# Moving one step's output products from the last single slot to the head of the first slot of two steps

## The chip, the core and the metric

The kernel runs on one core of a Trainium2 chip. The metric is the device time of one execution in microseconds (us). The engines are named as in the profile: PE is TensorE (matmuls; PEld its weight loads), DVE is VectorE, ACT is ScalarE, POOL is GpSimd, and SP is SyncE, which here issues most of the DMAs.

## The reference

Windowed attention with block summaries runs ahead of a gated network without a nonlinearity. What is computed:

```python
# q, k, v: (4, 8, 768, 64); block 32, window 16
k_sum = k.reshape(B, H, nb, block, D).max(axis=3)
v_sum = v.reshape(B, H, nb, block, D).mean(axis=3)
scores_l = scale * q @ k^T            # kept where |i - j| < window
scores_s = scale * q @ k_sum^T + log(block)
a = softmax(concat(scores_l, scores_s))
attn = a @ concat(v, v_sum)           # -> x: 3072 tokens x 512
a = x @ w1;  b = x @ w2               # 512 x 1024 each
out = ((a * b) @ w3) @ w_out          # 1024 x 1024, 1024 x 512
```

## The kernel before, in words

**Two streams of work share PE.** The attention is cut into 24 steps (6 units of 512 tokens by 4 pairs of heads). A step consists of its scores (`scores`, L383: 32 small matmuls into two PSUM banks), the masked minimum and the exponentials (`reduce` on DVE, L397; `expose` on ACT, L411), the normalization (`normalize` on ACT, L421), the transposes (`transposes`, L441: 16 matmuls into two banks), their copy to SBUF (`evacuate`, L449 and L451, both on ACT here), and the outputs (`outputs`, L464: 32 small matmuls into one bank), which `finish_step` follows with a copy out of PSUM (`keep_raw` on ACT, L484). The network is a stream of 128x512 matmuls (L128, and L747 for the products of a fast scheme with seven products instead of eight). `run` puts a given number of that stream's columns between the parts of the steps.

**The order on PE is the order in which the code calls.** PE, SP and POOL run in the order of the code; ACT and DVE do so inside the blocks marked `manual_schedule(engines=VECTOR)` for the calls of those blocks, while other work (weight casts, copies of the stream) is merged in by a scheduler. From step 8 on, steps 8 to 15 have a slot each (`lump`), and steps 16 to 23 go two to a slot (`two_steps`). In `lump(p)` the outputs of step p - 3 come first, then the transposes of p - 2 and the scores of p. In `two_steps(8)`, the first of its kind, come the transposes of step 14, whatever outputs of steps 12 and 13 are still open, and the scores of steps 16 and 17; the outputs of 14, the transposes and the outputs of 15 stand further down.

**PSUM banks.** Eight banks are dealt out in rings by tag: two for "mm", two for "tp", four for "sc". The ring "sc" holds the scores (two banks a step), the outputs of the later steps (`SPARE`), and every third accumulator of the network's second unit (`bank(wide)`). Just ahead of the place at hand the ring goes: outputs of step 12, two for the scores of 15, the accumulator `mm_2858`, outputs of 13, two for the scores of 16, two for the scores of 17. So the second bank of step 17's scores is the one that the outputs of step 13 had: PE may write it when the copy of L484 has read it.

**DMA lanes.** Each DMA issued by SP or ACT signals its landing on one of eight semaphores (`DMAHW0` to `DMAHW7` in the lists of order below), which the program deals out in turn. Before it issues a DMA, the issuing engine waits until the last DMA of that lane has landed; what stands behind on that engine waits too. On ACT this concerns `project`, which sends its results out from ACT (L562, behind the copy of L561).

**Values.** `load_values` (L332, three DMAs) and `fetch_means` (L366) fill a step's tile `v`, of which there are two; the loads of step 15 reuse the tile of step 13 and go when the outputs of 13 are through. The weights of the fast scheme stream in through `flow_in` (L792, tile `ws`).

Of the kernel before, what the change touches and what calls it, by code (L numbers as in the profile page):

```python
# [76 lines left out]
def attention_moe(ctx, tc, qG, kW, kT, vP, vW, vB, mask, w1, w2, w3T, wo, out, outT):  # L77
# [241 lines left out]
    def batches(u):  # L319

        for b in range(B):
            at, to = max(0, b * BLOCKS - u * NBLK), min(NBLK, (b + 1) * BLOCKS - u * NBLK)
            if at < to:
                yield b, slice(at, to), to - at

    def load_values(u, p):


        v = sb.tile([P, 2, NBLK, P], F32, name="v", bufs=2)

        for g, rows in ((0, slice(0, CUT)), (1, slice(0, CUT - 64)), (1, slice(CUT + NB - 64, KR))):
            (nc.gpsimd if u >= LAST_UNITS else nc.sync).dma_start(v[rows, g], vW[u, p, rows, g])  # L332
        return v
# [28 lines left out]
    def fetch_means(u, p, v):  # L362
        for b, blocks, n in batches(u):
            for g, at in enumerate((CUT, CUT - 64)):
                src = vS[b][32 * p : 32 * p + NB]
                nc.sync.dma_start(v[at : at + NB, g, blocks], src.unsqueeze(1).broadcast_to([NB, n, P]))  # L366
# [41 lines left out]
    def expose(h, sm, mx):  # L408
        for i in ORDER:
            j = h * NBLK + i  # L410
            nc.scalar.activation(  # L411
                sm[:, j], sm[:, j], AF.Exp, bias=mx[:, 0, j : j + 1], scale=-1.0, accum_out=mx[:, 1, j : j + 1]
            )
# [20 lines left out]
    def transposes(sm, **more):  # L434

        tp = [ps.tile([P, 512], F32, name="tp", **more or {"bufs": 2}) for _ in range(2)]
        for j in range(NI):
            for g in range(2):
                rows = slice(64 * g, 64 * g + 64)
                to, p = tp[g][:KR, j * 64 : j * 64 + 64], sm[rows, j]  # L440
                nc.tensor.transpose(to, p, ident[rows, rows])  # L441
        return tp

    def evacuate(tp, second="V", home=None):
        if home is None:
            pt = [sb.tile([KR, U], F32, name="pt", bufs=4) for _ in range(2)]
        else:
            pt = [home[:KR, g * U : (g + 1) * U] for g in range(2)]
        nc.scalar.copy(pt[0], tp[0][:KR, :U])  # L449
        if second == "A":  # L450
            nc.scalar.copy(pt[1], tp[1][:KR, :U])  # L451
        else:
            nc.vector.tensor_copy(pt[1], tp[1][:KR, :U])
        return pt
# [571 lines left out]
    def place(s):  # L1026
        return divmod(s, NPAIR)

    inputs, values, sms = {}, {}, {}

    def fetch(s):
        if s < NS:
            inputs[s] = load_scores(*place(s))

    def fetch_values(s):
        if s < NS:
            values[s] = load_values(*place(s))
# [5 lines left out]
    def fill(s):  # L1043
        if s < NS:
            gather(*place(s), inputs[s][1])

    def begin(s):
        u, p = place(s)
        held_in = sb.tile([P, 2 * U], F32, name="sm", tag="wf", bufs=6)
        sm = held_in[:, : NI * KR].rearrange("p (a b) -> p a b", b=KR)  # L1050
        mx = aligned([P, 3, NI], name="mx", bufs=4)
        sms[s] = sm, held_in
        return u, sm, mx, scores(*inputs.pop(s))
# [13 lines left out]
    def load_batch():  # L1067
        for _ in range(2 if later_batches else 0):
            load_, work = later_batches.pop(0)
            under_way.append((work, load_()))  # L1070

    def reduce_batch():
        for work, raw in under_way:
            work(raw)
        under_way.clear()
# [175 lines left out]
    def finish_step(p, pt, **more):  # L1251
        u, c = place(p)
        po = outputs(pt, values.pop(p), **more)
        if u < 2:
            keep_x(po, xs[u])
        else:
            keep_raw(po, u, c)
# [47 lines left out]
    def lump(p):  # L1305

        lag, last = p in LAG, p == SINGLE - 1
        if p == NFIRST:
            load_batch()
            fill(p)  # L1310
        else:
            if p not in LAG or p == LAG[0]:
                fetch_means(*place(p - 1), values[p - 1])
            elif p > LAG[1]:
                fetch_means(*place(p - 2), values[p - 2])
            fetch(p + 1)
        with tc.manual_schedule(engines=VECTOR):
            if p - 3 in turned:
                finish_step(p - 3, turned.pop(p - 3), **SPARE)
            t, home = sms.pop(p - 2)  # L1320
            turned[p - 2] = evacuate(transposes(t), "V" if p in (12, 13) else "A", home)
            u, sm, mx, sc = begin(p)
            reduce(u, 0, sc, sm, mx)
            if p > NFIRST + 1:
                expose(0, sm, mx)
                reduce(u, 1, sc, sm, mx)
        if last:
            fetch(p + 2)
        if lag and p > LAG[0]:
            fetch_values(p - 1)  # L1330
        run(given[0] + (24 if p == NFIRST + 1 else 18) * U)
        with tc.manual_schedule(engines=VECTOR):
            if not lag or last:
                finish_step(p - 2, turned.pop(p - 2), **SPARE)
            if p <= NFIRST + 1:
                expose(0, sm, mx)
                reduce(u, 1, sc, sm, mx)
            expose(1, sm, mx)
            invert(mx)
            normalize(sm, mx)  # L1340
            fill(p + 1)
            reduce_batch()
        if not lag or last:
            fetch_values(p)
        if last:
            fill(p + 2)
        for work in EXTRA.get(p, ()):
            work()
        run((given[0] + UP_TO[p]) / 2)
        load_batch()  # L1350
        run(UP_TO[p])
# [8 lines left out]
    def two_steps(m):  # L1360

        a, b = 2 * m, 2 * m + 1
        first = m == PAIRS[0]
        if first:
            for p in (a - 2, a - 1):
                fetch_means(*place(p), values[p])
        with tc.manual_schedule(engines=VECTOR):
            if first:
                t, home = sms.pop(a - 2)
                pt = evacuate(transposes(t), "A", home)  # L1370
            for p in (a - 4, b - 4):
                if p in turned:
                    finish_step(p, turned.pop(p), **SPARE)
            if m in PAIRS:
                (u, sm, mx, sc), (u2, sm2, mx2, sc2) = [begin(p) for p in (a, b)]
                reduce(u, 0, sc, sm, mx)
                expose(0, sm, mx)
                reduce(u, 1, sc, sm, mx)
        if not first:
            fetch_values(a - 2)  # L1380
        for work in LATER.get((m, 0), ()):
            work()
        if m in PAIRS:
            fetch(a + 2)
            run(given[0] + LEAD / 2)
            with tc.manual_schedule(engines=VECTOR):
                expose(1, sm, mx)
                reduce(u2, 0, sc2, sm2, mx2)
                invert(mx)
            run(given[0] + LEAD / 2)  # L1390
            with tc.manual_schedule(engines=VECTOR):
                if first:
                    finish_step(a - 2, pt, **SPARE)
                    turn((a - 1,), "A")
                expose(0, sm2, mx2)
                reduce(u2, 1, sc2, sm2, mx2)
                if m == PAIRS[0] + 1:
                    first_sums(0)
                normalize(sm, mx)
            if not first:  # L1400
                fetch_values(b - 2)
            fetch(b + 2)
            run(CLASSIC + LAST_SINGLE * FAST if first else (given[0] + begins(m + 1)) / 2)
            with tc.manual_schedule(engines=VECTOR):
                if first:
                    finish_step(a - 1, turned.pop(a - 1), **SPARE)
                expose(1, sm2, mx2)
                invert(mx2)
                normalize(sm2, mx2)
                if m == PAIRS[0] + 2:  # L1410
                    first_sums(1)
        if not first and m - 1 <= PAIRS[-1]:
            with tc.manual_schedule(engines=VECTOR):
                turn((a - 2, b - 2), "A")
        if m not in PAIRS:
            fetch_values(b - 2)
        for p in (a, b):
            fill(p + 2)
            if not first and p - 2 in values:
                fetch_means(*place(p - 2), values[p - 2])  # L1420
        for work in LATER.get((m, 1), ()):
            work()
        run(begins(m + 1))
# [75 lines left out]
```

## Time and profile before

| What | Value |
|---|---|
| Median of 3 runs | 505.38 us (505.33 to 505.58) |
| The profiled execution: its own time | 503.69 us |
| The profiled execution: its span, first to last instruction | 501.9 us |
| PE busy | 482.8 us, 96% of the span |
| ACT busy | 315.6 us, 63% |
| DVE busy | 358.4 us, 71% |

The span is 1.8 us short of the profiled execution's time, and that time is 1.7 us under the median of the runs without a profile. PE's busy share includes waits inside a run of matmuls, since their ends are modelled; how dense PE really is shows in the time from one group's start to the next one's.

### The profile page before, as it was taken

The numbers are of one execution on the slowest core, as the hardware profiler recorded it, in microseconds if no ns is written. First come the engines' busy times: TensorE is split into PE (matmuls) and PEld (weight loads), VectorE is DVE, ScalarE is ACT, GpSimd is POOL, SyncE is SP. The second block draws the span as 40 slices with busy tenths as digits, with TensorE's granted clock in tenths as the row PEclk, the third lists the DMA queues.
The fourth block names the chain that finished last, engine by engine and source line by source line (L and its number), as shares of the span: only waits on it lengthen the run. The fifth ranks groups of instructions, "written<-read, shape, count | busy, mean of one in ns | idle before, by whom it ended". The sixth has DMA issues, their size and how long they took to land.

```text
span 501.9 us, 10535 instructions
## 1 busy us (share of the span) xinstructions
PE 482.8 (96%) x3804; PEld 391.5 (78%) x3804; DVE 358.4 (71%) x874; ACT 315.6 (63%) x874; POOL 70.5 (14%) x131
## 2 busy tenths in 40 slices
PE   0998999999999999999999999999999999999997
PEld 0766778888877888888777888888888888888886
DVE  4879887897714798985559995799967038139972
ACT  5588965677816888887797779489534412413710
POOL 1024533000202110001252131202000000000000
PEclk9999999999999999999999999999999999999999
DMA  8999597999499999989999999997769656565762
GB/s 341 412 406 303 209 352 246 370 400 411 144 315 257 271 277 339 277 255 332 313 341 330 336 369 251 365 281 228 227 173 296 208 200 193 188 196 182 219 200 85
DMA packets 54404, 139.29 MB, mean 278 GB/s; under 512 B 6224, under 2 KB 17232, under 8 KB 51792
## 3 DMA queue, kind: packets, MB, share of 16 engines
q1 hardware_dynamic: 49136, 124.71, 73.1%
q0 software_dynamic: 4064, 11.82, 9.8%
q10 hardware_dynamic: 1152, 2.10, 1.1%
q8 instruction: 30, 0.49, 0.4%
q14 instruction: 22, 0.18, 0.1%
HBM read 105.89 MB, written 32.70 MB: 276 GB/s over the span
## 4 chain that ended last, share of the span: by engine, by line
PE 75%; DVE 9%; ACT 8%; DMA 5%; issue 1%; SPq 1%; ACTq 0%
PE ln L747 41%; PE mm L128 26%; PE po L464 4%; PE sc L383 3%; ACT sm L411 3%; DVE wf L211 2%; DVE w L124 2%; DMA ws<-wS 2%; DMA v<-vS 2%; PE tp L441 2%; ACT w L226 1%; ACT hT L650 1%; DMA k<-in_kW_dram 1%; DMA wraw<-in_wo_dram 1%; DVE wf L208 1%
## 5 line engine op out<-in xcount | busy, mean ns | idle before, releaser
L747 PE MATMUL ln<-xT,ws 128*128 128x512 f32 x672 | 156.7, 392 | 0.1
L747 PEld LDWEIGHTS ln<-xT,ws 128*128 128x128 f32 x672 | 125.0, 188 | 28.9 <-DVE tmp L767 0.8
L128 PE MATMUL mm<-x,w 128*128 128x512 f32 x384 | 89.5, 392 | 0.0
L128 PEld LDWEIGHTS mm<-x,w 128*128 128x128 f32 x384 | 71.4, 188 | 15.7 <-issue 0.8
L411 ACT ACTIVATE sm<-sm,mx 128x120 f32<-128x120 f32 x192 | 74.0, 393 | 11.7 <-DVE mx L397 11.6
L747 PE MATMUL ln<-hT,ws 128*128 128x512 f32 (+1 forms) x348 | 77.6, 383 | 0.1
L767 DVE TENSOR_TENSOR tmp<-ln,tmp 128x512 f32<-128x512 f32 (+1 forms) x53 | 35.6, 681 | 53.8 <-PE ln L747 39.7
L747 PEld LDWEIGHTS ln<-hT,ws 128*128 128x128 f32 x348 | 63.6, 188 | 13.3 <-ACT tmp L765 0.6
L128 PE MATMUL mm<-w,w 128*128 128x512 f32 x192 | 50.5, 414 | 14.7 <-ACT w L226 11.4
L650 ACT CAST hT<-hr 128x512 fp32r<-128x512 f32 x56 | 32.1, 625 | 40.7 <-DVE hr L824 32.0
L128 PEld LDWEIGHTS mm<-w,w 128*128 128x128 f32 x192 | 36.5, 196 | 25.6 <-ACT w L226 11.8
L397 DVE CUSTOM_DVE_ANT_0 sm<-sc,mask_sb 128x120 f32<-128x120 f32 x192 | 41.3, 278 | 15.3 <-PE sc L383 15.3
L128 PE MATMUL mm<-wp,h 128*128 128x512 f32 x192 | 45.7, 394 | 0.0
L128 PEld LDWEIGHTS mm<-wp,h 128*128 128x128 f32 x192 | 35.6, 188 | 8.3 <-issue 0.5
L421 ACT ACTIVATE sm<-sm,mx 128x120 f32<-128x120 f32 x128 | 39.3, 395 | 2.4 <-DVE mx L417 2.4
L124 DVE TENSOR_TENSOR hT<-hr,hT 128x512 fp32r<-128x512 f32 x56 | 35.9, 696 | 3.9 <-ACT hT L650 3.9
L411 ACT ACTIVATION_READ_ACCUMULATOR sm<-sm,mx 128x1 f32 x192 | 37.8, 197 | 0.0
L124 DVE TENSOR_TENSOR w<-wf,w 128x1024 fp32r<-128x1024 f32 (+1 forms) x22 | 26.4, 1200 | 8.0 <-ACT w L226 7.9
L226 ACT CAST w<-wf 128x1024 fp32r<-128x1024 f32 (+1 forms) x22 | 21.3, 969 | 15.6 <-DVE wf L211 14.3
L370 POOL COPY k<-ks 128x96 f32<-128x96 f32 (+1 forms) x32 | 11.2, 363 | 135.6 <-DMA k<-in_kW_dram 110.8
L765 ACT COPY tmp<-ln 128x512 f32<-128x512 f32 x32 | 18.8, 590 | 14.9 <-PE ln L747 13.7
L181 ACT ACTIVATE wf<-wraw 128x1024 f32<-128x1024 f32 (+1 forms) x22 | 23.1, 1061 | 6.6 <-DMA wraw<-in_wo_dram 3.6
(73 smaller groups left out, 578.5 us busy)
## 6 DMA issues: line engine op xcount, KB each, us to landing
ws<-wS SPq DMA_DIRECT2D x56, 512.0 KB
wraw<-in_w3T_dram SPq DMA_DIRECT2D x8, 1024.0 KB
wraw<-in_w_dram SPq DMA_DIRECT2D x8, 1024.0 KB
wS<-sp SPq DMA_DIRECT2D x16, 512.0 KB
ws<-pS SPq DMA_DIRECT2D x16, 512.0 KB
raw<-in_kT_dram SPq DMA_DIRECT2D x16, 392.0 KB
wS<-w SPq DMA_DIRECT2D x12, 512.0 KB
ws<-pW SPq DMA_DIRECT2D x24, 256.0 KB
```

Of the source, the lines that this page charges most:

```text
L124: eng.tensor_tensor(dst, src, hi.bitcast(F32), ALU.subtract)
L128: nc.tensor.matmul(acc, lhsT=a, rhs=b, start=first and i == 0, stop=last and i == len(terms) - 1)
L181: nc.scalar.activation(f[:, some], words[:, some, 1].bitcast(F32), AF.Prelu, scale=2.0**-112, alpha=-(2.0**32),)
L226: nc.scalar.copy(t[:, 0, some], f[:, some])
L397: nc.vector.tensor_tensor_reduce(out=sm[:, j], in0=sc[h][:, i * KR : (i + 1) * KR], in1=mask_sb[:, 0 if blk == 0 else 2 if blk == BLOCKS - ...
L411: nc.scalar.activation(sm[:, j], sm[:, j], AF.Exp, bias=mx[:, 0, j : j + 1], scale=-1.0, accum_out=mx[:, 1, j : j + 1])
L421: nc.scalar.activation(sm[:, j], sm[:, j], AF.Copy, scale=mx[:, 2, j : j + 1])
L464: nc.tensor.matmul(po[cols, at : at + 64], lhsT=v[:KR, g, i, cols], rhs=pt[g][:, (h * NBLK + i) * 64 : (h * NBLK + i + 1) * 64], start=Tru ...
L650: nc.scalar.copy(dst[0], src)
L747: nc.tensor.matmul(bank[:, cols], lhsT=x, rhs=y[:, cols], start=c + j == 0 and (split or k in o.first), stop=c == steps - 1 and j == 2 and ...
L765: nc.scalar.copy(parts[to][:, cols], got)
L767: nc.vector.tensor_tensor(parts[to][:, cols], got, parts[more][:, cols], ALU.add)
```

## The change

The outputs of step 13 leave `lump(15)`. They are done by the loop that stands in `two_steps(8)` behind the transposes of step 14, since step 13 is then still in `turned`. The values of step 15, whose tile is that of step 13, are loaded behind the scores of steps 16 and 17, and their means right behind them.

```diff
@@ lump(p)
         with tc.manual_schedule(engines=VECTOR):
-            if not lag or last:
+            if not lag:
                 finish_step(p - 2, turned.pop(p - 2), **SPARE)
...
-        if not lag or last:
+        if not lag:
             fetch_values(p)
@@ two_steps(m)
         if first:
-            for p in (a - 2, a - 1):
-                fetch_means(*place(p), values[p])
+            fetch_means(*place(a - 2), values[a - 2])
...
-        if not first:
+        if first:
+            fetch_values(a - 1)
+            fetch_means(*place(a - 1), values[a - 1])
+        else:
             fetch_values(a - 2)
```

On PE, around the end of `lump(15)` and the head of `two_steps(8)`, before: `mm` is the network's last accumulator ahead of the fast scheme, `po` outputs, `tp` transposes, `sc` scores, `ln` the fast scheme. The outputs of step 13 are `po_2993`, the second bank of step 17's scores is `sc_3123`.

```order
L128 MATMUL mm_2983<-wp1_77,h_2012 128x512 x3
L464 MATMUL po_2993<-sm_2598,v_2794 64x64 [waits DMAHW7_49,DMAHW4_49,Activation_49]
...
L128 MATMUL mm_2983<-wp2_78,h_2128 128x512 x3
...
L128 MATMUL mm_2983<-wp7_83,h_2536 128x512 x3
L441 MATMUL tp_3080<-ident_64,sm_2761 120x64 [waits PE_49]
...
L383 MATMUL sc_3102<-k_2881,q_2880 64x120 [waits DMAHW1_49,DVE_49,DMAHW2_49,PE_49,Pool_49]
...
L383 MATMUL sc_3123<-k_2959,q_2958 64x120 [waits Activation_49]
...
L747 MATMUL ln_3157<-xT_2801,ws_3039 128x512 [waits DMAHW3_49]
```

The same place on PE with the change; the outputs of step 13 are `po_3076`, the second bank of step 17's scores is `sc_3117`.

```order
L128 MATMUL mm_2983<-wp1_77,h_2012 128x512 x3
L128 MATMUL mm_2983<-wp2_78,h_2128 128x512 x3
...
L128 MATMUL mm_2983<-wp7_83,h_2536 128x512 x3
L441 MATMUL tp_3056<-ident_64,sm_2761 120x64 [waits Activation_49]
...
L464 MATMUL po_3076<-sm_2598,v_2794 64x64 [waits DMAHW7_49,DMAHW4_49]
...
L383 MATMUL sc_3096<-k_2881,q_2880 64x120 [waits DMAHW1_49,DVE_49,DMAHW2_49,PE_49,Pool_49]
...
L383 MATMUL sc_3117<-k_2959,q_2958 64x120 [waits Activation_49]
...
L747 MATMUL ln_3157<-xT_2801,ws_3017 128x512 [waits DMAHW3_49]
```

The 32 matmuls of `po` moved from inside the last accumulation to between the transposes and the scores; the wait of the last bank of scores for ACT is the wait for the copy that reads `po`.

On ACT, the same place before, from the copy of step 13's outputs (`po_2993`) to the copies of step 14's transposes (`tp_3080`, `tp_3081`):

```order
L484 COPY xraw_2903<-po_2993 128x512 [waits PE_49]
L411 ACTIVATE sm_2925,mx_2926<-sm_2925,mx_2926 128x120 [waits DVE_49] x4
L650 CAST xT_3356<-xraw_2233 128x512 [waits DVE_49]
...
L561 COPY o_3071<-mm_2983 128x512 [waits PE_49]
L421 ACTIVATE sm_2925<-sm_2925,mx_2926 128x120 x5
L562 DMA out_0_dram<-o_3071 128x512 [waits DMAHW0_49,Activation_49]
L449 COPY sm_2761<-tp_3080 120x512 [waits PE_49]
L451 COPY sm_2761<-tp_3081 120x512 [waits PE_49]
```

ACT with the change, from the last normalization of step 15:

```order
L421 ACTIVATE sm_2925<-sm_2925,mx_2926 128x120 x7
L686 CAST sp_3612<-wr_3028 128x512 [waits DMAHW3_49,DMAHW1_49,DMAHW4_49,DMAHW0_49,DVE_49]
L561 COPY o_3049<-mm_2983 128x512 [waits PE_49]
L686 CAST sp_3623<-wr_3028 128x512 [waits DMAHW2_49,DMAHW5_49,DMAHW0_49,DVE_49]
L562 DMA out_0_dram<-o_3049 128x512 [waits DMAHW5_49,Activation_49]
L449 COPY sm_2761<-tp_3056 120x512 [waits PE_49]
L451 COPY sm_2761<-tp_3057 120x512 [waits PE_49]
L484 COPY xraw_2903<-po_3076 128x512 [waits PE_49]
L650 CAST xT_3356<-xraw_2233 128x512 [waits DVE_49]
```

The copy of step 13's outputs moved from ahead of the DMA of L562 to behind it and behind the two copies of transposes. Two casts of weight sums (L686) moved ahead of that DMA. Its lane changed from `DMAHW0`, whose last user is the second `v<-vS` of step 14's values, to `DMAHW5`, whose last user is the load `ws_3023` (`ws_3045` before), the second half of the second product's weights.

On SP, before, from the load of `ws_3045` to the last means of step 15 (`v_3033`; `v_2962` are the values of step 14):

```order
L792 DMA ws_3045<-wS1_1_91 128x1024 [waits DMAHW5_49]
L366 DMA v_2962<-vS2_134 24x4x128 [waits DMAHW7_49]
L366 DMA v_2962<-vS2_134 24x4x128 [waits DMAHW0_49]
L792 DMA ws_3161<-wS2_0_94 128x1024 [waits DMAHW1_49]
L332 DMA v_3033<-in_vW_dram 96x512 [waits DMAHW6_49,DMAHW2_49,PE_49]
...
L366 DMA v_3033<-vS2_134 24x4x128 [waits DMAHW5_49]
L366 DMA v_3033<-vS2_134 24x4x128 [waits DMAHW6_49]
```

SP with the change (`v_3147` are the values of step 15):

```order
L792 DMA ws_3023<-wS1_1_91 128x1024 [waits DMAHW5_49]
L366 DMA v_2962<-vS2_134 24x4x128 [waits DMAHW6_49]
L366 DMA v_2962<-vS2_134 24x4x128 [waits DMAHW0_49]
L792 DMA ws_3161<-wS2_0_94 128x1024 [waits DMAHW1_49]
L792 DMA ws_3163<-wS2_1_95 128x1024 [waits DMAHW2_49]
...
L332 DMA v_3147<-in_vW_dram 96x512 [waits DMAHW7_49,DMAHW6_49,PE_49]
...
L366 DMA v_3147<-vS2_134 24x4x128 [waits DMAHW1_49]
L366 DMA v_3147<-vS2_134 24x4x128 [waits DMAHW2_49]
```

Up to the load on `DMAHW5` nothing moved on SP. In the list before, the first `v_3033<-vS2_134` is the next DMA on `DMAHW5`. The five loads of step 15's values moved down, past one load of weights and two stores, and the last one now stands on the lane of `ws_3163`.

## Rows read from the trace of the kernel before

**Rows 1.** The page: its head, the engines' busy times, and the engines' shares of the chain that ended last.

```profile
span 501.9 us, 10535 instructions
...
PE 482.8 (96%) x3804; PEld 391.5 (78%) x3804; DVE 358.4 (71%) x874; ACT 315.6 (63%) x874; POOL 70.5 (14%) x131
...
PE 75%; DVE 9%; ACT 8%; DMA 5%; issue 1%; SPq 1%; ACTq 0%
```

**Rows 2.** The timeline of PE from the end of `lump(14)` to the outputs of step 15: start, length, engine, line, operation, tiles, form, count. A row's end is modelled; the distance to the next row's start is what it cost.

```profile
224.63 4.24 PE L128 MATMUL mm<-wp,h 128*128 128x512 f32 x18
228.80 1.15 PE L464 MATMUL po<-sm,v 120*64 120x64 f32 x32
229.89 0.69 PE L441 MATMUL tp<-ident,sm 64*120 64x64 f32 x16
230.50 1.05 PE L383 MATMUL sc<-k,q 64*64 64x120 f32 x32
231.48 4.38 PE L128 MATMUL mm<-wp,h 128*128 128x512 f32 x18
235.79 1.15 PE L464 MATMUL po<-sm,v 120*64 120x64 f32 x32
236.87 4.38 PE L128 MATMUL mm<-wp,h 128*128 128x512 f32 x18
241.18 0.68 PE L441 MATMUL tp<-ident,sm 64*120 64x64 f32 x16
241.79 1.87 PE L383 MATMUL sc<-k,q 64*64 64x120 f32 x64
243.59 4.87 PE L747 MATMUL ln<-xT,ws 128*128 128x512 f32 x18
248.39 1.15 PE L464 MATMUL po<-sm,v 120*64 120x64 f32 x32
...
255.11 1.44 PE L464 MATMUL po<-sm,v 120*64 120x64 f32 x32
256.48 5.75 PE L747 MATMUL ln<-xT,ws 128*128 128x512 f32 x23
```

**Rows 3.** The timeline of ACT over the same stretch; in brackets the idle time ahead of an instruction and what ended it. ACTq is ACT's sequencer, which issues a DMA.

```profile
235.29 0.34 ACTq L562 DMA_DIRECT2D out_dram<-o  x1
236.99 0.59 ACT L484 COPY xraw<-po 128x512 f32<-128x512 f32 x1 [1.73 <-PE po L464]
...
241.36 0.57 ACT L561 COPY o<-mm 128x512 f32<-128x512 f32 x1
241.83 1.54 ACT L421 ACTIVATE sm<-sm,mx 128x120 f32<-128x120 f32 x5
245.76 0.34 ACTq L562 DMA_DIRECT2D out_dram<-o  x1
246.15 0.59 ACT L449 COPY sm<-tp 120x512 f32<-120x512 f32 x1 [2.77 <-DMA v<-vS]
246.63 0.59 ACT L451 COPY sm<-tp 120x512 f32<-120x512 f32 x1
247.11 0.41 ACT L411 ACTIVATE sm<-sm,mx 128x120 f32<-128x120 f32 x1
...
251.61 0.63 ACT L686 CAST sp<-wr 128x512 fp32r<-128x512 f32 x1
```

**Rows 4.** The timeline of SP over the same stretch: issues of DMAs, those of one kind that follow each other in one row.

```profile
232.23 2.87 SPq L792 DMA_DIRECT2D ws<-wS  x2
235.14 3.17 SPq L366 DMA_DIRECT2D v<-vS  x2
239.83 0.34 SPq L792 DMA_DIRECT2D ws<-wS  x1
240.42 3.04 SPq L332 DMA_DIRECT2D v<-in_vW_dram  x3
244.72 0.75 SPq L366 DMA_DIRECT2D v<-vS  x2
...
257.68 0.79 SPq L792 DMA_DIRECT2D ws<-wS  x2
```

**Rows 5.** The chain of waits through this stretch, in order of time: start, length, what.

```profile
229.59 8.37 DMA ws<-wS
...
237.98 7.71 DMA v<-vS
...
256.55 8.22 PE ln L747 x33
```

**Rows 6.** Busy times by stretch: the stretch, its length, PE, PEld, DVE, ACT and POOL busy (instructions), PE's granted clock as a share of 2.4 GHz, the DMA share, GB/s. The first is the longest wait inside the stream of matmuls once it runs, the others are the end of the program.

```profile
43.00:46.00 3.00, 1.70 (x28) 1.07 (x21) 3.00 (x5) 3.00 (x5) 1.68 (x2) 1.00 1.06 401
...
496.00:498.20 2.20, 2.16 (x18) 1.95 (x17) 0.45 (x3) 0.00 (x0) 0.00 (x0) 1.00 0.36 140
498.20:501.20 3.00, 0.00 (x0) 0.00 (x0) 0.42 (x1) 0.00 (x0) 0.00 (x0) 1.00 0.21 72
501.40:501.90 0.50, 0.00 (x0) 0.00 (x0) 0.00 (x0) 0.00 (x0) 0.00 (x0) 0.50 0.00 0
```

**Rows 7.** The timeline of PE: an early run of the same 128x512 matmuls, soon after PE's first instruction.

```profile
12.40 5.21 PE L128 MATMUL mm<-w,w 128*128 128x512 f32 x13 [0.21 <-DVE w L124]
```

## The prediction

> **What bounds the kernel now.** I read the page first: PE is busy for 96% of the span and carries 75% of the chain that ended last [rows 1]. Then PE's timeline over the stretch that the change touches [rows 2]: each group starts where the one before it stops, so there is no open gap; what PE loses it loses inside a group. I measure that by starts. Eighteen matmuls of 512 columns in mid-run cost 228.80 - 224.63 = 4.17 us (232 ns each); behind a group of small matmuls they cost 4.31 (231.48 to 235.79, and 236.87 to 241.18) [rows 2]. So PE sets the end, and anything that holds it is paid in full, unless a later wait of PE shrinks by as much. Third, ACT beside it [rows 3]: it is not the bound, but it stood still for 2.77 us up to 246.15, right behind the issue of a DMA at 245.76. Fourth, SP and the chain of waits, for the reason: that DMA sits on the lane of a `v<-vS` that was issued at 237.98 and landed 7.71 us later, at 245.69 [rows 4, 5]. ACT's issue followed the landing by 0.07 us. DMAs here take 8 us from issue to landing, and an ACT that meets a busy lane waits for them.
>
> **The change part by part: what it takes away.** The 32 output matmuls cost 1.08 us in their old place (235.79 to 236.87) and 1.09 in front of transposes (228.80 to 229.89) [rows 2]: the work itself is the same. What goes is one break of the long run, 4.31 - 4.17 = 0.14 us. Without any wait PE would begin the transposes of step 14 at 241.18 - 1.08 - 0.14 = 239.96, the outputs of 13 at 240.57 (the transposes cost 241.79 - 241.18 = 0.61), the scores of 16 at 241.66, and those of 17 half of 243.59 - 241.79 = 1.80 later, at 242.56 [rows 2]. On ACT the wait of 1.73 us for those outputs goes too [rows 3]; ACT isn't the bound there, so I count nothing for it, but it matters for when ACT arrives, next.
>
> **What it adds: a wait in the middle of step 17's scores.** The second bank of these scores is that of step 13's outputs, so PE needs the copy of L484. Before, that copy began at 236.99, some 5 us ahead of need [rows 3]. Now it is the third copy behind ACT's DMA. ACT came to that DMA at 246.15 - 2.77 = 243.38; it will come earlier, by the 1.73 us of wait, by the copy (0.48) and by a cast that moved behind, later by two casts that moved ahead (0.63 each, as the one at 251.61): 243.38 - 1.73 - 0.48 + 0.63 = 241.8 [rows 3]. The DMA's lane is now that of the second load of the second product's weights. When it lands is read from SP: the next user of this lane was the first `v<-vS` issued at 244.72, which stands behind three loads whose issues ended at 240.42 + 3.04 = 243.46 [rows 4]. So it waited, and the load landed at about 244.7, or 10 us behind its own issue (the second of the two from 232.23, which ended at 235.10) [rows 4]. Everything on SP up to that load is unmoved, so I keep 244.7. Then, by the distances in ACT's rows: first copy 0.46 behind the landing (245.69 to 246.15), second 0.48 later, L484 another 0.48 later, and 0.59 for itself [rows 3, 5]: 244.65 + 0.46 + 0.48 + 0.48 + 0.59 = 246.66. PE goes on at 246.7 instead of 242.56, a wait of **4.14 us**. Behind the waiting matmul is all of PE's queue, the fast scheme's stream first. DVE and ACT hang on it with the minima and exponentials of steps 16 and 17, which are needed 40 us later.
>
> **What it gives back.** PE's run from 243.59 costs 4.80 against 4.31 for the same eighteen [rows 2]: 0.49 lost in it, at the place where a bank waits for ACT's late copies of transposes. With PE 4 us behind and ACT not, that is gone. So is 0.29 of the outputs at 255.11, which cost 1.37 against 1.08 [rows 2]. The 33 matmuls from 256.55 cost 8.22 against 33 x 0.232 = 7.66 [rows 5], 0.56 lost in several small waits; some may go as well. I take 0.49 + 0.29 = 0.78, with 0.49 and 1.34 as ends.
>
> **What is moved and should cost nothing.** The values of step 15 go later. Their last means wait for a load of weights that now goes at 240.4 in place of the first value load; with the 8.37 and 7.71 us of the two DMAs in the chain [rows 4, 5] it lands at 248.8 and the means at 256.5. PE needs them at 255.11 + 3.2 = 258.3: hidden, by 1.8 us, and only because PE is late. The load of the fourth product's weights, issued at 257.68 before [rows 4], waits for those means' landing too, and so hardly moves.
>
> **The sum.** 4.14 - 0.14 - 0.78 = +3.22 us on PE's path. The profiled execution's 503.69 would become 506.9, the span 505.1, and the median 505.38 + 3.2 = **508.6 us**. Its own range: landing 0.7 earlier and 1.34 given back, 4.14 - 0.70 - 0.14 - 1.34 = +1.96 (507.3); landing 0.7 later and 0.49 given back, 4.14 + 0.70 - 0.14 - 0.49 = +4.21 (509.6). The 0.7 is my allowance for DMAs that take 7.7 to 8.4 us in neighbouring rows [rows 5].
>
> **Rival 1: the clock falls in the wait.** At the end of the program the granted clock was still 1.00 (2.4 GHz) over the 3.00 us of idle PE from 498.20, and 0.50 (1.2 GHz) from 501.40 on; an idle stretch of 1.3 us at 43 to 46 left it at 1.00 [rows 6]. A wait of 4.14 us is longer than either. That speaks for it; against it stands that one fall is all that the trace shows, and that the idle time ahead of a fall need not be the same each time. The price: early in the program 13 matmuls took 5.21 us, 401 ns each against 232 [rows 2, 7], so a slow stretch loses 42% of its length; with the whole 5.21 us that is 2.2 us, and little if the clock returns at once. I take the middle of 0.3 and 2.2, 1.3: **509.9 us**, up to 510.8. The Trainium skill, page "TensorE: Matmul & The Clock Gate", section "What's actually happening", holds that half rate is TensorE's resting state and that it comes back only with sustained work; by that rule the wait ends in a slow stretch, and this case would be the likely one. The end of this trace agrees that idleness lowers the clock.
>
> **Rival 2: no wait to speak of.** If the lane's load has landed when ACT arrives at 241.8, L484 ends at 241.8 + 0.48 + 0.48 + 0.59 = 243.35 and PE waits 0.8 us: 0.8 - 0.14 - 0.78 = -0.1, **505.3 us**, not slower. It decides at a landing of about 242.4, where the sum still is within 1 us. Against it: SP's issue at 244.72, 2.3 us later [rows 4], and the 2.77 us that ACT stood at the same kind of wait [rows 3].
>
> **Rival 3: the values of step 15 are late.** If the two DMAs in a row take 2 us more each than in the chain, the means land at 260.5 and PE waits 2 us at the outputs of step 15, beside the forecast's wait: **510.6 us**. For it: the margin of 1.8 us. Against it: fewer bytes are ahead of them than before, because the value loads went behind.
>
> **How the numbers follow.** Forecast 0.52, rival 1 0.36, rival 3 0.06, rival 2 0.06. The likeliest is 508.6. The range goes from the forecast's low end, 507.3, to 511.0, which takes in rival 1 with its upper price and most of rival 3; rival 2 and the tails stay out. A measurement can tell about 0.2% here, 1.0 us. Slower by more than that are the forecast, rival 1 and rival 3, less a little for a lane that comes much earlier: 0.94. Within it: 0.05. Faster: 0.01.
>
> **What would show it.** In the changed kernel's profile PE's timeline must have an idle stretch of some 4 us inside the scores of steps 16 and 17, at 242.6 to 246.7, released by ACT's copy of L484; ACT must show its idle time behind the casts and ahead of L449, ended by a DMA; the outputs of step 15 must follow their neighbours without the 0.29. A granted clock under 1.00 behind the wait would show rival 1; a wait at the outputs of step 15 rival 3. The prediction is wrong if PE's wait is under 2 us, or if the waits further down, which I count as 0.78, give back the most of it.

## The result and the profile after

| | kernel before | changed kernel |
|---|---|---|
| median, us | 505.36 | 509.81 |
| runs, us | 504.15 to 505.58 | 508.00 to 511.12 |
| ratio, 95% interval | 1 | 1.0096 (1.0067 to 1.0126) |
| profiled execution: time, span, us | 503.69, 501.9 | 510.04, 508.3 |
| granted clock, mean of the span | 0.999 | 0.993 |

The changed kernel is slower by some 0.96%, 4.9 us by the ratio and 4.45 by the medians. 508.6 was the likeliest time, 507.3 to 511.0 the range; 509.9 was the time of rival 1.

The timeline of PE in the changed kernel (start, length, what; in brackets the idle time ahead and what ended it), beside [rows 2]:

```profile
231.61 8.46 PE L128 MATMUL mm<-wp,h 128*128 128x512 f32 x36
240.00 0.68 PE L441 MATMUL tp<-ident,sm 64*120 64x64 f32 x16
240.61 1.15 PE L464 MATMUL po<-sm,v 120*64 120x64 f32 x32
241.70 1.24 PE L383 MATMUL sc<-k,q 64*64 64x120 f32 x34
247.01 1.87 PE L383 MATMUL sc<-k,q 64*64 64x120 f32 x30 [4.08 <-ACT xraw L484]
248.81 5.98 PE L747 MATMUL ln<-xT,ws 128*128 128x512 f32 x18
254.72 1.15 PE L464 MATMUL po<-sm,v 120*64 120x64 f32 x32
255.80 0.69 PE L441 MATMUL tp<-ident,sm 64*120 64x64 f32 x16
256.42 5.05 PE L747 MATMUL ln<-xT,ws 128*128 128x512 f32 x21
261.40 1.15 PE L464 MATMUL po<-sm,v 120*64 120x64 f32 x32
262.48 13.21 PE L747 MATMUL ln<-xT,ws 128*128 128x512 f32 x57
275.63 1.87 PE L383 MATMUL sc<-k,q 64*64 64x120 f32 x64
```

The open gap is in the middle of the scores, two matmuls into those of step 17, and ACT's copy L484 ends it. Then look at the two rows behind the gap: 30 small matmuls take 1.80 us by starts, and 18 long ones 5.91, where [rows 2] has 4.80. No gap is open there. PE itself is slow. The granted clock tells it (by stretch, columns as in [rows 6]; the eighth figure is the clock):

```profile
244.00:245.00 1.00, 0.00 (x0) 0.00 (x0) 0.00 (x0) 0.00 (x0) 0.33 (x1) 1.00 1.00 344
245.40:245.60 0.20, 0.00 (x0) 0.00 (x0) 0.00 (x0) 0.20 (x1) 0.00 (x0) 0.52 0.91 369
251.00:252.00 1.00, 1.00 (x4) 0.71 (x4) 0.53 (x1) 0.23 (x2) 0.39 (x2) 0.50 0.99 325
252.20:252.40 0.20, 0.20 (x2) 0.16 (x2) 0.00 (x0) 0.20 (x2) 0.00 (x0) 0.92 1.12 420
```

The clock falls to 0.50 (1.2 GHz) at 245.4, in the wait, and is back at 1.00 (2.4 GHz) from 252.2. ACT over the same time, beside [rows 3], and the chain of waits that leads to it, beside [rows 5]:

```profile
240.89 0.62 ACT L686 CAST sp<-wr 128x512 fp32r<-128x512 f32 x1
245.01 0.34 ACTq L562 DMA_DIRECT2D out_dram<-o  x1
245.39 0.59 ACT L449 COPY sm<-tp 120x512 f32<-120x512 f32 x1 [3.88 <-DMA ws<-wS]
245.88 0.59 ACT L451 COPY sm<-tp 120x512 f32<-120x512 f32 x1
246.35 0.60 ACT L484 COPY xraw<-po 128x512 f32<-128x512 f32 x1
```

```profile
236.23 8.70 DMA ws<-wS
...
245.01 0.34 ACTq L562
...
246.47 0.50 ACT xraw L484
```

A load of weights issued at 236.23 lands 8.70 us later, at 244.94. ACT issues its DMA 0.07 behind that, and the three copies follow. Where the time went, by starts from PE's rows of both kernels:

| stretch | before | after | difference |
|---|---|---|---|
| start of the long run (chance, ahead of the change) | 231.48 | 231.61 | +0.13 |
| the long run, without the outputs of 13 | 8.62 | 8.39 | -0.23 |
| the outputs of 13 | 1.08 | 1.09 | +0.01 |
| transposes and scores, without the outputs of 13 | 2.41 | 7.72 | +5.31 |
| stream, first 18 | 4.80 | 5.91 | +1.11 |
| outputs, transposes, stream to the outputs of 15 | 6.72 | 6.68 | -0.04 |
| outputs of 15 | 1.37 | 1.08 | -0.29 |
| stream up to the scores of step 18 | 13.96 | 13.15 | -0.81 |
| sum, at the scores of step 18 | 270.44 | 275.63 | +5.19 |

PE's last matmul ends 6.36 us later than before, at 504.52. Most of what is added behind this table is one stop in the scores of a later pair, which the trace puts down to "issue", that is, to nothing that it shows:

```profile
328.62 1.45 PE L383 MATMUL sc<-k,q 64*64 64x120 f32 x44
331.76 0.83 PE L383 MATMUL sc<-k,q 64*64 64x120 f32 x20 [1.70 <-issue]
```

No other profile of the changed kernel or its variants has it. I take it for chance: this execution lies above the kernel's usual +4.5.

### The profile page after: what moved, and what is told of

The parts are those of the page before. It is cut to its first block, busy times and chain, and to the rows that moved or that the text cites. A ratio compares the mean times of both kernels' runs of the same rounds, so it can differ in the third digit from the quotient of the medians.

```text
span 508.3 us, 10532 instructions
## 1 busy us (share of the span) xinstructions
PE 483.7 (95%) x3804; PEld 394.0 (78%) x3804; DVE 359.3 (71%) x874; ACT 316.4 (62%) x874; POOL 71.2 (14%) x131
## 4 chain that ended last, share of the span: by engine, by line
PE 75%; DVE 10%; ACT 7%; DMA 6%; issue 2%; ACTq 0%; SPq 0%
PE ln L747 46%; PE mm L128 21%; PE po L464 3%; PE sc L383 3%; ACT sm L411 2%; DVE wf L211 2%; DVE w L124 2%; DMA ws<-wS 2%; PE tp L441 2%; DMA raw<-in_vB_dram 1%; DMA raw<-in_kT_dram 1%; ACT w L226 1%; DMA wraw<-in_wo_dram 1%; DVE wf L208 1%; ACT sm L421 1%
## 5 line engine op out<-in xcount | busy, mean ns | idle before, releaser
L747 PE MATMUL ln<-xT,ws 128*128 128x512 f32 x672 | 156.9, 394 | 0.0
L747 PEld LDWEIGHTS ln<-xT,ws 128*128 128x128 f32 x672 | 126.6, 190 | 27.5 <-issue 0.8
L747 PE MATMUL ln<-hT,ws 128*128 128x512 f32 (+1 forms) x348 | 77.3, 383 | 0.0
L747 PEld LDWEIGHTS ln<-hT,ws 128*128 128x128 f32 x348 | 63.7, 188 | 12.8
L383 PE MATMUL sc<-k,q 64*64 64x120 f32 x768 | 26.0, 274 | 5.8 <-ACT xraw L484 4.1
```

Of the source, the lines that this page charges most:

```text
L383: nc.tensor.matmul(sc[h][64 * g : 64 * g + 64, i * KR : (i + 1) * KR], lhsT=q[rows, i * P + 64 * g : i * P + 64 * g + 64], rhs=k[rows, i, ...
L747: nc.tensor.matmul(bank[:, cols], lhsT=x, rhs=y[:, cols], start=c + j == 0 and (split or k in o.first), stop=c == steps - 1 and j == 2 and ...
```

## The experiments

The kernel before varied on the chips of these runs from 501.6 to 508.4 us in nearly all of its runs. So the ratios decide where they can, and the rows of the profiled executions where the ratios can't.

| kernel | median, us | before beside it | ratio (95%) |
|---|---|---|---|
| changed, L562 by POOL | 506.60 | 504.98 | 1.0023 (0.9993 to 1.0053) |
| before, L562 by POOL | 505.04 | 504.98 | 1.0001 (0.9967 to 1.0035) |
| changed, outputs in a bank of mm | 507.46 | 504.98 | 1.0049 (1.0024 to 1.0073) |
| changed, wait filled, small matmuls | 509.37 | 504.98 | 1.0088 (1.0063 to 1.0113) |
| changed, wait filled, long matmuls | 507.53 | 504.64 | 1.0063 (1.0036 to 1.0091) |
| changed, outputs ahead of transposes | 508.44 | 504.64 | 1.0067 (1.0039 to 1.0094) |
| changed, scores of 17 later | 510.07 | 504.64 | 1.0099 (1.0072 to 1.0126) |
| changed, again | 509.91 | 504.57 | 1.0094 (1.0063 to 1.0125) |
| before, all three by POOL | 506.44 | 504.57 | 1.0040 (1.0015 to 1.0065) |
| changed, all three by POOL | 503.77, 502.82, 505.34 | 504.64, 504.57, 504.89 | 0.9990 (0.9965 to 1.0015), 0.9959 (0.9937 to 0.9981), 0.9990 (0.9959 to 1.0021) |

**Is it ACT at the lane?** The theory: PE waits because L484 stands behind a DMA issue whose lane is busy. The first rival: the move itself costs. The second: the values of step 15, loaded later, cost. One line in the changed kernel takes ACT away from the lane:

```diff
-  nc.scalar.dma_start(out[u * U + t * P : u * U + (t + 1) * P], o)
+  eng = nc.gpsimd if u == 1 and t == NBLK - 1 else nc.scalar
+  eng.dma_start(out[u * U + t * P : u * U + (t + 1) * P], o)
```

> The changed kernel, but the last result DMA of the second unit (L562) is issued by POOL, not by ACT. Theory 1 (ACT, which stands at the busy lane of that DMA, makes PE wait for its copy L484): ACT reaches the three copies at about 241.8, L484 ends at about 243.2, PE's wait of 4.1 to 4.3 us shrinks to some 0.5 us, the clock stays at 1.00, and the waits given back further down (0.8) and the break saved (0.14) remain: 505.0 us (504.3 to 505.6). Theory 2 (the move itself is what costs: transposes, outputs and two steps' scores in one row keep PE waiting whoever issues the DMA): PE still waits 3 us or more, 508 us or more. Theory 3 (the values of step 15, loaded later, are the cost): 508 us or more, with a wait at the outputs of step 15.

PE's timeline of that kernel (it has one line more, so that L748 is L747 of the others):

```profile
243.10 1.04 PE L383 MATMUL sc<-k,q 64*64 64x120 f32 x30 [0.33 <-ACT xraw L484]
244.08 4.39 PE L748 MATMUL ln<-xT,ws 128*128 128x512 f32 x18
...
256.50 1.27 PE L464 MATMUL po<-sm,v 120*64 120x64 f32 x32 [1.35 <-DMA v<-vS]
257.70 10.50 PE L748 MATMUL ln<-xT,ws 128*128 128x512 f32 x45
270.34 3.01 PE L748 MATMUL ln<-xT,ws 128*128 128x512 f32 x12 [2.15 <-DMA ws<-wS]
```

The wait for L484 falls from 4.08 to 0.33, and in this execution the clock stays at 1.00: the theory holds, and the first rival falls. But 505.0 was expected and the median is 506.6. The last three rows show part of why: PE waits for the means of step 15 and for a load of the fourth product's weights. They are not the whole, since the profiled execution, with both waits in it, took 505.56, inside what was expected. Six of the twelve runs show a mean clock of 0.997 or less and took 506.35 to 511.41; the other six took 502.95 to 507.21. No profile shows where the clock fell in them.

Nor is it shown that the second rival had been hidden by the wait that I took away. The means that PE waits for here were issued at 248.32 and landed 7.93 us later, by the chain of waits. In the changed kernel the first of the two was issued at 246.85, and by the trace's record of landings both were there by 253.72, ahead of the 255.15 at which PE came for them here. So the values are late in this execution because they came later, and not only because PE was on time. The same edit in the kernel before:

> The kernel before, with the same DMA issued by POOL. Theory 1: ACT's stand of 2.77 us up to 246.15 goes; PE hardly waited for it (0.49 inside the run from 243.59, perhaps 0.29 at the outputs of step 15), so 504.7 us (504.3 to 505.3). If ACT's stand costs the kernel before nothing at all: 505.4. Theory 2 and 3 say nothing else of it: 505.4.

No difference that can be measured. In its profile ACT's stand is gone, and PE's first 18 of the stream take 4.34 by starts instead of 4.80; PE then waits 0.34 and 0.43 elsewhere. By the scores of step 18 it is 0.35 us ahead of the kernel before (38.61 against 38.96 from the start of the long run), less than these runs can tell.

**Is it the bank?** The outputs of step 13 get a bank of the other ring, and the scores of 17 need not wait:

```diff
-  finish_step(p, turned.pop(p), **SPARE)
+  finish_step(p, turned.pop(p), **({"tag": "mm", "bufs": 2} if first else SPARE))
```

> The changed kernel, but the outputs of step 13 go to a bank of the other ring (mm, two banks), so that the scores of step 17 need no bank that L484 has to empty; the second accumulator of the fast scheme's stream needs it instead, some 2.3 us later. Theory 1: PE does the scores of 17 at once (until about 243.5), starts the stream and waits there for L484, which still ends near 247.0: a wait of about 2 us instead of 4.3, the clock stays at 1.00, 506.6 us (506.0 to 507.5). Theory 2 (the lane decides nothing, the scores of 17 wait for something else): a wait of 4 us in the scores as before, 509 us or more. Theory 3 (values late): 509 us.

```profile
242.05 1.87 PE L383 MATMUL sc<-k,q 64*64 64x120 f32 x64
243.85 1.66 PE L747 MATMUL ln<-xT,ws 128*128 128x512 f32 x6
248.11 4.62 PE L747 MATMUL ln<-xT,ws 128*128 128x512 f32 x12 [2.60 <-ACT xraw L484]
```

The scores run through. The wait stands where the bank is needed next, 2.60 long instead of 4.08, although the lane came free a us later (246.04). The clock fell here too, over 249.05 to 252.5, which was not expected:

```profile
249.00:250.00 1.00, 1.00 (x4) 0.77 (x3) 1.00 (x11) 1.00 (x4) 0.00 (x0) 0.54 1.02 412
```

The median is 0.9 above the 506.6 that was expected, still within the range given with it. That the clock makes this difference is not shown: the profiled execution, in which it fell, took 506.31.

**Half of the move.** The outputs of step 13 stand ahead of the transposes, so that L484 is the first copy behind the DMA:

```diff
-  if first:
-      t, home = sms.pop(a - 2)
-      pt = evacuate(transposes(t), "A", home)
   for p in (a - 4, b - 4):
       if p in turned:
           finish_step(p, turned.pop(p), **SPARE)
+  if first:
+      t, home = sms.pop(a - 2)
+      pt = evacuate(transposes(t), "A", home)
```

> Half of the move: the outputs of step 13 still stand at the head of the slot of two steps, but ahead of the transposes of step 14, not behind them. ACT's copy L484 is then the first behind the DMA at the lane, not the third. Theory 1: L484 ends two copies (2 x 0.48) earlier, PE waits 3.3 to 3.4 us instead of 4.3, the second half of the loss stays: 1 us below the changed kernel in the place itself, 508.4 to 509.2 with a clock that falls all the same, 507 if it does not. If the place behind the transposes were the cause: no wait to speak of, 505.4.

508.44, as expected, and the loss is mostly still there. PE's row and ACT's:

```profile
247.96 1.87 PE L383 MATMUL sc<-k,q 64*64 64x120 f32 x30 [3.70 <-ACT xraw L484]
```

```profile
247.32 0.58 ACT L484 COPY xraw<-po 128x512 f32<-128x512 f32 x1 [4.52 <-DMA ws<-wS]
```

ACT's `L484` is now the first copy behind the DMA, and PE waits 3.70 us for it, behind a lane that came free at 246.86. So the place behind the transposes is not the cause; it adds two copies of 0.48 us.

**What does the clock cost?** Two kernels keep PE at work in the wait. One computes the scores of step 16 five times into the same place; the other does 17 long matmuls that nobody reads:

```diff
-  def scores(q, k):
+  def scores(q, k, times=1):
-  for i in range(NBLK):
+  for i in list(range(NBLK)) * times:
-  return u, sm, mx, scores(*inputs.pop(s))
+  return u, sm, mx, scores(*inputs.pop(s), times=5 if s == 16 else 1)
```

```diff
-  (u, sm, mx, sc), (u2, sm2, mx2, sc2) = [begin(p) for p in (a, b)]
+  u, sm, mx, sc = begin(a)
+  if first:
+      spare = ps.tile([P, 512], F32, name="mm", bufs=2)
+      for _ in range(17):
+          nc.tensor.matmul(spare, lhsT=wp[0][:, 0, :P], rhs=wp[0][:, 1, :512], start=True, stop=True)
+  u2, sm2, mx2, sc2 = begin(b)
```

> The changed kernel, but the scores of step 16 are computed five times over, into the same place: 64 more matmuls, some 3.6 us of small matmuls on PE in the time in which it would stand. It parts the wait from the clock. If the wait of 4.3 us costs by itself and the fall of the granted clock (0.50 from 245.4 to 252.2) costs some 2.7 to 3 us more because PE stands idle: PE goes on at 247.0 as in the changed kernel, the idle rest is under 1 us, the clock stays at 1.00 over 245 to 253, and the time is 505.4 + 4.3 - 0.14 - 0.78 = 508.8 less what the profile's own differences are, 508.2 to 508.9, below the changed kernel by 1 us or more and with less scatter. If the clock falls for another reason (the kind of matmuls, or chance): it falls here too, and the time is that of the changed kernel, 509.8.

> The changed kernel with 17 matmuls of 512 columns, whose result nobody reads, between the scores of step 16 and those of step 17: PE does some 3.9 us of the long kind of matmul in the time in which it would stand. In the run that filled this time with small matmuls the clock still fell, behind an idle rest of 1.48 and 0.47 us. If it is the standing PE that costs the clock: the rest of the wait is 0.3 to 1.5 us, the clock stays at 1.00 over 245 to 256, and the time is that of the kernel before plus the wait less what comes back, 4.3 - 0.14 - 0.78 = 3.4: 508.4 (507.8 to 509.0), below the changed kernel by 1 to 2.5 us. If the clock falls with any rest of idle time here: as the run with small matmuls, about 509.4. If it falls by chance, whatever PE does: as the changed kernel, 509.8.

> The changed kernel as it is, beside the kernel before on the chip of these runs. Ratio 1.007 to 1.012, most runs with a granted clock of 0.993 (a fall of some 7 us) and a few with 0.997; runs with 0.997 some 1.5 us below those with 0.993. Against it stands the run with PE kept at long matmuls, 1.0063 with a clock of 1.00: the difference is what the clock costs, 1.3 to 2.5 us.

The first edit adds 128 small matmuls, not the 64 that its expectation names; the 3.6 us there are those of 128. PE's timeline with the small matmuls, and its clock from the stretches:

```profile
241.57 4.51 PE L383 MATMUL sc<-k,q 64*64 64x120 f32 x162
247.56 0.63 PE L383 MATMUL sc<-k,q 64*64 64x120 f32 x12 [1.48 <-ACT xraw L484]
248.66 0.92 PE L383 MATMUL sc<-k,q 64*64 64x120 f32 x18 [0.47 <-issue]
249.51 5.85 PE L747 MATMUL ln<-xT,ws 128*128 128x512 f32 x18
```

```profile
249.30:249.40 0.10, 0.10 (x3) 0.00 (x0) 0.10 (x1) 0.00 (x0) 0.00 (x0) 0.50 1.06 395
252.60:252.80 0.20, 0.20 (x2) 0.14 (x1) 0.20 (x4) 0.20 (x3) 0.00 (x0) 0.81 0.98 257
```

PE's timeline with the long ones, and a stretch behind the wait:

```profile
244.43 4.15 PE L1378 MATMUL mm<-wp 128*128 128x512 f32 x17
248.51 0.42 PE L383 MATMUL sc<-k,q 64*64 64x120 f32 x2
250.73 1.04 PE L383 MATMUL sc<-k,q 64*64 64x120 f32 x30 [1.81 <-ACT xraw L484]
251.71 4.38 PE L747 MATMUL ln<-xT,ws 128*128 128x512 f32 x18
```

```profile
253.00:254.00 1.00, 1.00 (x6) 0.83 (x5) 1.00 (x6) 1.00 (x7) 0.93 (x3) 1.00 1.00 394
```

With the small matmuls the clock still fell, at 249.3, with 1.48 and 0.47 us of idle time left; I had expected it to stay. With the long ones it stayed: behind 1.81 us of idle time the next 30 and 18 matmuls take 0.98 and 4.31 by starts, where the changed kernel has 1.80 and 5.91. The price of the clock, read in the same rows, is 0.82 + 1.60 = 2.4 us. Against the same rows with the long matmuls it is 2.9 us in the profile of the changed kernel again (a wait of 3.92 us) and 2.5 in that of the outputs ahead of the transposes (3.70). Run by run the mean clock agrees: 0.999 or 1.00 in ten of eleven runs with long matmuls, 0.992 or 0.993 in all six of the changed kernel again. In times it is weaker: 1.0094 against 1.0063 is 1.6 us, and the intervals overlap. Two of the eight runs with small matmuls had a clock of 1.00 and were no faster (509.15, 509.89), and the profiled execution with the long ones, at a clock of 1.00, took 510.50, 3 us above its kernel's median. So other things move these runs as well, and the price rests on the rows.

**Scores of 17 later.** Here the scores of step 17 stand behind the first 18 of the stream, so that PE needs the bank 4.2 us later:

```diff
-  (u, sm, mx, sc), (u2, sm2, mx2, sc2) = [begin(p) for p in (a, b)]
+  u, sm, mx, sc = begin(a)
...
   run(given[0] + LEAD / 2)
   with tc.manual_schedule(engines=VECTOR):
       if first:
+          u2, sm2, mx2, sc2 = begin(b)
           finish_step(a - 2, pt, **SPARE)
           turn((a - 1,), "A")
+          reduce(u2, 0, sc2, sm2, mx2)
```

> The changed kernel, but the scores of step 17 stand behind the 18 stream matmuls that followed them, so that PE needs L484's bank some 4.2 us later; ACT still stands at the lane and all DMAs go as in the changed kernel. Theory 1 (only PE's wait for that bank costs): PE works through, meets the bank at 246.8 to 247 just when it comes free, waits under 0.7 us (more if the lane lands later than 245), the clock stays at 1.00; the waits at the values of step 15 and at the fourth product's weights, which showed as 1.35 and 2.15 us when ACT's stand was taken away, come back here, because PE is early again: 505.5 to 507.5. Theory 2 (ACT's stand costs by more than this bank): 508 or more.

A miss: 510.07, no better than the change. PE's timeline:

```profile
247.24 4.53 PE L747 MATMUL ln<-xT,ws 128*128 128x512 f32 x12 [2.78 <-ACT o L561]
251.70 1.05 PE L383 MATMUL sc<-k,q 64*64 64x120 f32 x32
...
256.72 0.65 PE L441 MATMUL tp<-ident,sm 64*120 64x64 f32 x15 [2.68 <-DVE mx L397]
```

It waits for nothing at L484, but twice elsewhere. The second wait is of my own making: the minima of step 17, moved behind, hold the bank of the next transposes. The first is ACT again, which in this execution stood at the lane of the DMA before (issued at 242.42, against 236.18 in the changed kernel). The clock fell at both, from 247.1 to 250.5 and from 257.3 to 260.7. The run does not tell the theories apart.

**Without any lane in the way.** The values and means of step 15 go to POOL as well, in the changed kernel and in the kernel before:

```diff
-  (nc.gpsimd if u >= LAST_UNITS else nc.sync).dma_start(v[rows, g], vW[u, p, rows, g])
+  (nc.gpsimd if u >= LAST_UNITS or (u, p) == place(15) else nc.sync).dma_start(v[rows, g], vW[u, p, rows, g])
...
-  nc.sync.dma_start(v[at : at + NB, g, blocks], src.unsqueeze(1).broadcast_to([NB, n, P]))
+  (nc.gpsimd if (u, p) == place(15) else nc.sync).dma_start(v[at : at + NB, g, blocks], src.unsqueeze(1).broadcast_to([NB, n, P]))
```

> The changed kernel with the last result DMA of the second unit and the values and means of step 15 issued by POOL, so that neither ACT nor these values stand behind a lane of SP's. Theory: PE waits under 0.6 us for L484, the values land by 250 to 254, before PE needs them at 254.9, and the clock stays at 1.00; what is left of the change is the break saved and the earlier waits gone: 504.5 (503.5 to 505.3), below the kernel before by up to 0.5 us if anything. If the moved values are not what made PE wait 1.35 us at the outputs of step 15 in the run with only ACT freed: that wait stays, 505.5 to 506.6. If the fourth product's weights are late for a reason of their own (2.15 us in that run): 506 or more with the wait there alone.

> The changed kernel with the last result DMA of the second unit and the values and means of step 15 issued by POOL, once more, beside the same edits on the kernel before. 503.8 to 504.4; ratio to the kernel before 0.997 to 1.000. If it is clearly below the kernel before and the same edits without the move are not, the move is worth its 0.14 us and more when nothing waits at a lane.

> The changed kernel with the last result DMA of the second unit and the values and means of step 15 issued by POOL, a third time, because the two measurements of it, ratios of 0.999 and 0.9959 to the kernel before, leave open whether it is faster. If it is faster by what the rows gave (0.23 us for the break, some 0.5 in the stream's first run, 0.29 at the outputs of step 15, up to 0.8 in the run behind them, less 0.3 to 0.5 us of wait for L484): ratio 0.996 to 0.999, and the three together below 1. If the second measurement was chance: 1.000 or above.

> The kernel before with the same three things issued by POOL as in the run with all of them (last result DMA of the second unit, values and means of step 15). It tells what the move itself is worth once nothing stands at a lane. If the move has a gain of its own, it is the break of the long run, 0.14 us, and this kernel is that much slower than the changed kernel with the same edits: 504.0 to 504.6 against 503.8 to 504.4 there. If the gain over the kernel before comes from POOL's issues alone, the two are alike and both below the kernel before by 0.5 to 1 us (its 0.49 in the run from 243.59 and 0.29 at the outputs of step 15).

PE's timeline of the changed kernel so edited, second measurement:

```profile
243.39 1.04 PE L383 MATMUL sc<-k,q 64*64 64x120 f32 x30 [0.52 <-ACT xraw L484]
244.36 4.42 PE L748 MATMUL ln<-xT,ws 128*128 128x512 f32 x18
...
250.41 5.05 PE L748 MATMUL ln<-xT,ws 128*128 128x512 f32 x21
255.39 1.15 PE L464 MATMUL po<-sm,v 120*64 120x64 f32 x32
256.47 13.21 PE L748 MATMUL ln<-xT,ws 128*128 128x512 f32 x57
```

The wait at the outputs of step 15 is gone, in this execution and in the first (which still waited 1.57 us for the fourth product's weights). So the late values were a second cost of the kernel with L562 alone moved to POOL. The third measurement's profiled execution took 970.95 us, as one of the kernel before beside it did (971.06), and no rows are read from it. Weighted by their intervals, the three ratios give 0.9976, with half an interval of 0.0015: the version beats the changed kernel by some 1.2%, and is some 0.2% under the kernel before, with 1 just outside the interval and inside two of the three. The same POOL edits without the move are slower than the kernel before, 1.004, which I had not expected. PE's row there:

```profile
267.51 5.71 PE L748 MATMUL ln<-xT,ws 128*128 128x512 f32 x24 [2.03 <-DMA ws<-wS]
```

2.03 us is what that wait costs in its one profile, and seven of its twelve runs show a mean clock of 0.997 or less, as do four of the twelve with L562 alone by POOL in the kernel before, and three of the 23 runs of the kernel before beside it. Whether the order of DMAs with POOL's or the chip's scatter does it is open.

## Why the prediction held, and what failed in it

- **The wait in step 17's scores (+4.14).** Right in place, releaser and size: from 241.70 to 247.01 pass 5.31 us, 4.33 more than the 0.98 of one step's scores, L484 ends the wait, and the lane came free at 244.94 where 244.7 was put. That this agrees to a quarter of a microsecond is partly luck: the load, whose place on SP had not moved, was issued at 236.23, 1.5 us later than before (234.75), and then took 8.70 us instead of the 10 that the prediction read. Taking ACT off the lane leaves 0.33.
- **The break saved (-0.14).** Mis-sized a little: 0.23.
- **What comes back (-0.78).** Right in kind, too small: 0.29 at the outputs of step 15 as said; the 0.49 in the stream's first run comes out as 1.60 less 1.11; and in the long run behind it 0.81, where I had said that "some may go as well" of 0.56 and counted none. Together that is 1.59, above the upper end of 1.34.
- **The values of step 15, hidden.** Right: no wait in the changed kernel, and rival 3 did not occur. The margin was mis-sized: the last means landed at 253.7 and not at 256.5, and PE came for them at 261.40. So the reason "only because PE is late" is not borne out in this execution. With L562 by POOL they landed at 256.25 and later, close to what was forecast, and cost 1.35 us.
- **The clock.** This is the step that failed: the prediction gave the steady clock 0.52 and the fall 0.36. The clock fell in the profiled execution, and all six runs of the changed kernel measured again show a mean of 0.992 or 0.993. Rival 1 was the case; its mechanism was right, and its price, 1.3, was mis-sized: 2.4. The upper end, 2.2, assumed a slow stretch of 5.2 us of PE's time; PE ran from 247.01 to 252.2 in it, which is just that. I took the middle of the range where even the upper end was a little short. The Trainium skill, page "TensorE: Matmul & The Clock Gate", section "What's actually happening", calls the throttled clock the default, which activity releases; by that rule a slow stretch behind the wait was to be expected, and the rows of 245.4 to 252.2 agree. The rows of the kernel before pointed the same way: in [rows 6] the clock fell behind some 3.2 us of idle PE, and the forecast wait was longer. Against them I set only that one fall is all that the trace shows, and that the idle time ahead of a fall need not be the same each time.
- **The sum.** 4.14 - 0.14 - 0.78 was to be +3.22. Of the table's +5.19, 0.13 is chance and 2.4 the clock, which leaves +2.65 for the forecast's own terms. The larger clock and the larger give-back cancelled in part, so that the median came within 0.1 us of rival 1's 509.9 is luck.
- **Rival 2** did not occur: the lane landed 2.5 us behind the point from which it decides.

## What to carry to other kernels

Before an evacuation is moved behind other work, look at what stands ahead of it in the queue of the engine that does it: a DMA issue that waits for its lane holds back every copy behind it, and the reader of the bank pays. A wait of PE of several us has a second price, the clock behind it, here 2.4 to 2.9 us behind waits of 3.7 to 4.1. And a wait that is taken away can uncover the next one: price what it may hide before counting the gain.

## What the runs showed of the hardware

How long PE stood does not by itself tell whether the clock falls. It fell with 4.08 us of idle time, at 245.4, still in the wait; with 2.60 us, at 249.05, when PE had been at work again for 0.9 us; with 2.78 and 2.68 us in the run with the scores of 17 later; and with 1.48 and 0.47 us behind 4.5 us of small matmuls, at 249.3. It did not fall with 1.81 us behind 17 long matmuls, nor with 1.35 and 2.15 us in the run with L562 on POOL. The slow stretch was 6.8 us in the first case, as in the two other profiles with waits of 3.70 and 3.92 us, and some 3.4 us in the rest. What else decides is open.
